# Spreading quadrant maxima as f32r high and low parts, at the end of a burst, in an induced-attention and maxout kernel

## Chip, cores and metric

The kernel runs on one core of one Trainium2 chip. The metric is the device time in microseconds of one execution; a lower number is better. The engines are named as in the profile: PE is TensorE (PEld its weight loads), DVE is VectorE, ACT is ScalarE, POOL is GpSimd, and SP issues DMAs.

## What is computed

Four batches of 12544 tokens with 128 channels go through two attention stages with 32 inducing rows, and the result through a maxout layer with three weight matrices and an output matrix. Everything is float32.

```python
B, N, m, C = (4, 12544, 32, 128)
def mab(q, kv):
    s = scale * (q @ kv.transpose(0, 2, 1))
    s = s - s.max(-1, keepdims=True)
    a = np.exp(s)
    a /= a.sum(-1, keepdims=True) + 1e-09
    return a @ kv
h = mab(I, x)              # 32 inducing rows attend over 12544 tokens
x = mab(x, h)              # 12544 tokens attend over 32 states
h = np.maximum(np.maximum(x @ w1, x @ w2), x @ w3)   # d_ff = 768
return h @ w_out
```

The first call of `mab` is called first attention here, the second one second attention.

## The kernel before

A batch is 98 tiles of 128 tokens: group 0 has 2 tiles, groups 1 to 6 have 16 each. The first attention of a group has its scores in one PSUM bank of 128 partitions: the tokens are split into four quadrants, and each quadrant holds the 32 inducing rows in its own 32 partitions. So an inducing row has four maxima, one in each quadrant, and they have to be put together before the exponential. `attend_max` (L292, VectorE) takes the negated maximum along each partition (`mq`, 128x1). `attend_column` (L299, ScalarE) multiplies the 0/1 matrix `quad` (128x4) with it (`md`, 128x4: the maximum stands in the column of its quadrant). `attend_spread` (L306, TensorE) is a float32 matmul of `md` with the 0/1 matrix `sel` (128x128), which gives every partition all four maxima of its inducing row. `attend_least` (L312, or L315 and L316) takes the least of the four and, from group 1 on, of the group before. Then come the exponential (`attend_weights`, L322, ScalarE), the factor for the older sums (`attend_scale`, L365), a transposition of 32x32 blocks (`attend_transpose`, L336, VectorE), and in a later burst the sums over tokens (`attend_sums`, L346, 16 pairs of small matmuls).

Batch 0's first attention is a phase of its own (`phase1_first`). After it, everything runs in slots, 150 a batch. A slot is one column block of 128 of the 768 maxout columns for one chunk of 512 tokens (256 in group 0). In slot s, `advance` issues on TensorE one product of slot s+1 (`pu`, L669) and one of slot s (`pv`, L675); ScalarE keeps max(pu, 0) (`ru`, L684) and rounds an older result to f32r (`hi`, L691); VectorE takes max(pv, ru) (`h`, L702); the rest `lo` = h - hi is made on GpSimd (L699), or on VectorE (L705) for the slots of a group of 24 that `LOWVEC` names, two slots later and behind that slot's `h`. `stage2` issues, six slots behind, the three products with the output matrix (L727 to L729, `hi` and `lo` with its high and low parts; one more, L726, at the start of a chunk). The banks `pu` and `pv` exist twice each: slot s+2 overwrites slot s. A float32 product on this kernel's operands with 4 or 512 columns shows as two records each in the profile; an f32r product is one.

While batch b goes through the slots, the first attention of batch b+1 (called n in the code) is laid between them by the table `plan`: `at(s, f, ...)` puts a function behind `advance` of slot s and before its `stage2`. s0 is the first slot of the group g, which has 24 slots. `burst(s0 + 2, *first)` puts several matmul groups side by side: scores of the second attention of batch b (`scores_products`, L585), scores of the first attention of batch n (`attend_products`, L282) and the sums of the group before (`attend_sums`). There is a second burst at s0 + 15 in some groups. `softmax1(n, g, s, wait)` lays the steps from the maximum to the transposition at s+2 to s+10, with s = s0 + 2 after a first burst; `wait` (0, or `LATE` = 12) moves the steps from the spread on. The order in which the code calls these is the order on each engine: all five engines run a hand-written order.

```python
at(s + 2, attend_max, b, gi)
at(s + 3, attend_column, b)
at(s + 6 + wait, attend_spread, b)
at(s + 7 + wait, attend_least, b, gi)
at(s + 8 + wait, attend_weights, b, gi)
```

Per batch n = 1, 2, 3 there are seven spreads: groups 0 and 1 from g = 1 (its first and second burst), groups 2, 3 and 4 from the first bursts of g = 2, 3 and 4, group 5 from the second burst of g = 4, and group 6 from the first burst of g = 5.

Of the kernel before, what the change touches and what calls it, by code (L numbers as in the profile page):

```python
# [8 lines left out]
F32 = mybir.dt.float32  # L9
F32R = mybir.dt.float32r  # L10
# [3 lines left out]
ALU = mybir.AluOpType  # L14
AX = mybir.AxisListType
# [10 lines left out]
def kernel(ctx, tc, x, xt, ind_t, w1, w2, w3, w_out, out):  # L26
    nc = tc.nc
# [3 lines left out]
    P = 128  # L31
    NT = N // P
    NJ = DF // P
    NQ = P // M
# [18 lines left out]
    ORDER = "a a a a b a a b 0 c d m b a b a b a p d b 1 c s b b b s S m b q 2 c s 3 c s d s s d s"  # L53
    STEPS2 = (3, 5, 7, 8, 9, 10, 11, 13, 14, 15)
    scale = 1.0 / float(C) ** 0.5
    LATE = 12
    LOWVEC = (23, 0, 15, 18)
    LOWLAST = (23, 0, 9, 15, 18)
    UW = 2 * DF + C
    UQ = UW // NQ  # L60
# [4 lines left out]
    while t0 < NT:  # L65
        nt = NT % GT if t0 == 0 and NT % GT else GT
        assert nt == GT or nt <= NQ
        g = dict(t0=t0, nt=nt, at=t0 * P)
        groups.append(g)
        t0 += nt  # L70
    NG = len(groups)

    const = ctx.enter_context(tc.tile_pool(name="const", bufs=1))
    xp = ctx.enter_context(tc.tile_pool(name="xp", bufs=2))
    xtp = ctx.enter_context(tc.tile_pool(name="xtp", bufs=7))
    wk = ctx.enter_context(tc.tile_pool(name="wk", bufs=2))
    bp = ctx.enter_context(tc.tile_pool(name="bp", bufs=2))
    hp = ctx.enter_context(tc.tile_pool(name="hp"))
    op = ctx.enter_context(tc.tile_pool(name="op", bufs=2))
# [3 lines left out]
    bank_a, bank_u, bank_v, bank_o = (  # L83
        [ps.tile([P, 512], F32, name=f"{n}{i}", tag=f"{n}{i}") for i in range(2)] for n in ("aux", "pu", "pv", "acc")
    )

    spare = [None]
# [37 lines left out]
    def first_loads():  # L125
# [11 lines left out]
    sel = const.tile([P, P], F32, name="sel")  # L137
    nc.vector.tensor_reduce(
        out=sel[:, :M], in_=ident.rearrange("p (q m) -> p m q", m=M), axis=AX.X, op=ALU.add
    )  # L140
    nc.vector.tensor_copy(
        out=sel[:, M:].rearrange("p (q m) -> p q m", m=M),
        in_=sel[:, :M].unsqueeze(1).to_broadcast([P, NQ - 1, M]),
    )
    quad = const.tile([P, NQ], F32, name="quad")
    nc.vector.tensor_reduce(out=quad, in_=ident.rearrange("p (q m) -> p q m", m=M), axis=AX.X, op=ALU.add)

# [90 lines left out]
    state = {}  # L238
# [63 lines left out]
    def attend_spread(b, bank=None):  # L302
# [2 lines left out]
        st["mp"] = bank or spare[0]  # L305
        nc.tensor.matmul(out=st["mp"][:, :NQ], lhsT=sel, rhs=st["md"], start=True, stop=True)  # L306

    def attend_least(b, gi):
        st = state[b]
        new, mp = st["mneg"][:, gi : gi + 1], st["mp"]  # L310
        if b == 0 or gi == 0:
            nc.vector.tensor_reduce(out=new, in_=mp[:, :NQ], axis=AX.X, op=ALU.min)  # L312
        else:

            nc.vector.tensor_reduce(out=mp[:, NQ : NQ + 1], in_=mp[:, :NQ], axis=AX.X, op=ALU.min)  # L315
            nc.vector.tensor_tensor(out=new, in0=mp[:, NQ : NQ + 1], in1=st["mneg"][:, gi - 1 : gi], op=ALU.min)  # L316

    def attend_weights(b, gi):
        w = groups[gi]["nt"] * M
# [78 lines left out]
    def phase1_first():  # L398
# [19 lines left out]
        half(1, 0)  # L418
        attend_spread(0, bank_o[0])
        attend_least(0, 0)  # L420
        half(1, 8)
        work(WORK[0])
        st = state[0]
        for gi in range(NG - 1):
            last = gi == NG - 2
            attend_products(0, gi + 1, bank_a[(gi + 1) % 2])
            attend_weights(0, gi)
            half(gi + 2, 0)
            attend_max(0, gi + 1)
            attend_column(0)  # L430
            half(gi + 2, 8)
            if gi > 0:
                attend_sums(0, gi - 1, bank_o[1])
                attend_keep(0, gi - 1)
            attend_transpose(0, gi)
            if not last:
                work(WORK[gi + 1][0])
            attend_spread(0, bank_o[0])
            attend_least(0, gi + 1)
            if gi == 3:  # L440
                transpose_w2()
            if last:
                prep_products()
            else:
                work(WORK[gi + 1][1])
# [261 lines left out]
    class Chunk:  # L707
# [7 lines left out]
        def low(self, k):  # L715

            if self.q is None or (self.gi == 1 and self.q == k == 0):
                return False
            return NJ * self.q + k in (LOWVEC if self.b + 1 < B else LOWLAST)

# [49 lines left out]
    def at(s, f, *args):  # L770
        plan[s].append((f, args))

    def softmax2(b, gi, *when):

        gen = []

        def step():
            if not gen:
                gen.append(scores_steps(b, gi))
            next(gen[0], None)  # L780

        for s in when:
            at(s, step)

    def softmax1(b, gi, s, wait=0):

        at(s + 2, attend_max, b, gi)
        at(s + 3, attend_column, b)
        at(s + 6 + wait, attend_spread, b)
        at(s + 7 + wait, attend_least, b, gi)  # L790
        at(s + 8 + wait, attend_weights, b, gi)
        if gi > 0:
            at(s + 9 + wait, attend_scale, b, gi)
        at(s + 10 + wait, attend_transpose, b, gi)

    def burst(s, *what):

        for f, *args in what:
            at(s, f, *args)

    for b in range(B):
        base = b * per_batch + short
        n = b + 1
        for g in range(1, NG):
            s0 = base + (g - 1) * WIN
            first, second = [], []
            if g + 1 < NG:

                if n == B:

                    if g % 2:
                        first += [(scores_products, b, k, bank_a[k % 2]) for k in (g + 1, g + 2) if k < NG]
                elif b > 0 or g > 1:
                    first.append((scores_products, b, g + 1, bank_a[0]))
                softmax2(b, g + 1, *(s0 + i for i in STEPS2))
            if n < B:

                if g == 1:
                    if n == 1:
                        at(s0 + 1, load_tokens, 1, 4)  # L820
                    at(s0 + 4, load_channels, n, 2)
                    first.append((attend_products, n, 0, bank_a[1]))
                    softmax1(n, 0, s0 + 2)
                    second += [(attend_products, n, 1, bank_a[1]), (attend_sums, n, 0)]
                    at(s0 + 16, attend_add, n, 0)
                    softmax1(n, 1, s0 + 15)
                    at(s0 + 16, load_tokens, n + 1, 0)
                    at(s0 + 20, load_channels, n, 3)
                elif g < NG - 2:
                    first += [(attend_products, n, g, bank_a[1]), (attend_sums, n, g - 1)]  # L830
                    at(s0 + 3, attend_add, n, g - 1)
                    softmax1(n, g, s0 + 2, 0 if g == NG - 3 else LATE)
                    at(s0 + 4, load_channels, n, g + 2)
                    more = g + 3
                    if more < NG:
                        at(s0 + 5, load_tokens, n, more)
                    else:
                        at(s0 + 5, load_tokens, n + 1, more - NG + 1)
                    if g == NG - 3:
                        second += [(attend_products, n, g + 1, bank_a[1]), (attend_sums, n, g)]  # L840
                        at(s0 + 16, attend_add, n, g)
                        softmax1(n, g + 1, s0 + 15)
                        at(s0 + 16, load_tokens, n + 1, 2)
                elif g == NG - 2:
                    first += [(attend_products, n, g + 1, bank_a[1]), (attend_sums, n, g)]
                    at(s0 + 3, attend_add, n, g)
                    softmax1(n, g + 1, s0 + 2)
                    at(s0 + 5, load_tokens, n + 1, 3)
                    second.append((attend_sums, n, g + 1))
                    at(s0 + 16, load_tokens, n + 1, 4)  # L850
                    at(s0 + 16, attend_add, n, g + 1)
                    at(s0 + 18, add_quadrants, ("state", n), bank_a[1])
                    at(s0 + 18, total_sums, ("state", n), bank_a[0])
                    at(s0 + 19, invert_total, ("state", n))
                    at(s0 + 19, combine_states, ("state", n), 1)
                    at(s0 + 21, combine_products, ("state", n), bank_a[0])
                    at(s0 + 22, combine_high, ("state", n))
                    at(s0 + 23, combine_low, ("state", n))
                    for r in range(NQ):
                        at(s0 + 25 + 3 * r, combine_rows, ("state", n), r)  # L860
                else:
                    first += [(scores_products, n, 1, bank_a[0]), (scores_products, n, 0, bank_a[1])]
                    softmax2(n, 1, *(s0 + i for i in STEPS2))
                    softmax2(n, 0, *(s0 + i for i in (4, 6, 8, 9, 10, 11, 12, 13, 14, 15)))
                    if n + 1 < B:
                        at(s0 + 18, start_batch, n + 1)
                        at(s0 + 18, load_channels, n + 1, 0)
                        at(s0 + 18, load_channels, n + 1, 1)
            burst(s0 + 2, *first)
            burst(s0 + 15, *second)  # L870
# [25 lines left out]
    with tc.manual_schedule(engines=MANUAL):  # L896
        phase1_first()
        st = state[0]
# [89 lines left out]
```

## Time and profile before

| | |
|---|---|
| time, three runs | 822.32, 822.78 (median), 823.0 us |
| span of the profiled execution | 821.3 us, 1.5 us under the median of the runs |
| granted clock of TensorE | 1.000 over the span |
| batch 0's first attention, before the slots | up to about 48 us |
| POOL | 650.1 us busy (79%) |
| DMA | 102.51 MB, mean 125 GB/s, 38.5% of 16 engines' time |

The page gives of each engine the busy time as a share of the span, and then the chain of work that ended last, followed back from the last instruction; its share of an engine says how much of the end that engine set. The profiled execution's own time is known by its span. In rows in order of time the columns are the start, the duration in us, engine, line, operation, output <- input, tile and form, and the count; in square brackets stands the idle time of the engine before it and what ended that.

### The profile page before, as it was taken

To read this page: it belongs to the slowest core of one execution; us is meant where nothing else is said; L and a number is where in the kernel's file an instruction comes from. 1 tells how busy PE (TensorE), PEld (TensorE's weight loads), DVE (VectorE), ACT (ScalarE), POOL (GpSimd) and SP (SyncE) were. 2 spreads that over 40 slices of the span, in tenths; PEclk is the share of its full clock that TensorE was granted. 3 is DMA by queue.
4 is the path that set the end of the run, shared out by engine and by line. 5 is a ranking of instruction groups with operands and counts; after the bars stand their busy time and mean duration, and the time that the engine had idled before them with its cause. 6 is when DMAs were issued, how large, how long until landed. Compare 5 with 4: busy or idle time off the path is not lost.

```text
span 821.3 us, 14725 instructions
## 1 busy us (share of the span) xinstructions
PE 809.0 (98%) x4604; PEld 634.0 (77%) x4604; DVE 627.4 (76%) x1090; ACT 743.5 (91%) x1558; POOL 650.1 (79%) x521
## 2 busy tenths in 40 slices
PE   7989999999999999999999999999999999999998
PEld 5757778778788787777778777877778788787886
DVE  4977778777787687787786877877778788778864
ACT  5779889898899898898999988989889899899996
POOL 1269779778799697787888977977879889888887
PEclk9999999999999999999999999999999999999999
DMA  8844534433443544344334352431223222222221
GB/s 325 310 137 151 188 88 161 161 120 107 136 139 121 154 154 162 84 162 159 110 106 142 116 205 83 159 119 58 63 80 89 71 78 77 65 81 76 63 78 52
DMA packets 44206, 102.51 MB, mean 125 GB/s; under 512 B 9568, under 2 KB 13536, under 8 KB 38880
## 3 DMA queue, kind: packets, MB, share of 16 engines
q1 hardware_dynamic: 43984, 101.44, 38.5%
q8 instruction: 37, 0.61, 0.3%
q14 instruction: 41, 0.34, 0.1%
q10 hardware_dynamic: 144, 0.13, 0.0%
HBM read 48.12 MB, written 25.69 MB: 90 GB/s over the span
## 4 chain that ended last, share of the span: by engine, by line
PE 95%; DMA 2%; DVE 1%; SPq 1%; ACT 1%; issue 0%; ACTq 0%; DVEq 0%
PE acc L727 17%; PE pv L675 16%; PE acc L728 16%; PE acc L729 16%; PE pu L669 16%; PE aux L585 3%; PE acc L726 3%; PE acc L346 3%; PE aux L282 2%; DMA xg<-in_x_dram 2%; PE acc L306 0%; PE pu L272 0%; SPq L100 0%; PE pv L272 0%; PE aux L551 0%; DMA pT<-pl 0%
## 5 line engine op out<-in xcount | busy, mean ns | idle before, releaser
L699 POOL TENSOR_TENSOR lo<-h,hi 128x512 fp32r<-128x512 f32 (+1 forms) x502 | 634.9, 1295 | 129.8 <-ACT hi L691 84.0
L702 DVE TENSOR_TENSOR h<-pv,ru 128x512 f32<-128x512 f32 (+1 forms) x600 | 404.2, 675 | 167.8 <-PE pv L675 81.2
L684 ACT ACTIVATE ru<-pu 128x512 f32<-128x512 f32 (+1 forms) x600 | 375.3, 626 | 52.6 <-PE pu L669 49.7
L691 ACT CAST hi<-h 128x512 fp32r<-128x512 f32 (+1 forms) x600 | 386.4, 644 | 0.4 <-DVE h L702 0.3
L727 PE MATMUL acc<-hi,wo_hi 128*128 128x512 f32 (+1 forms) x600 | 236.9, 395 | 0.0
L675 PE MATMUL pv<-pT,us 128*128 128x512 f32 (+1 forms) x600 | 232.1, 387 | 0.3 <-DVE h L702 0.3
L669 PE MATMUL pu<-pT,us 128*128 128x512 f32 (+1 forms) x600 | 231.5, 386 | 0.4 <-DMA pT<-pl 0.4
L728 PE MATMUL acc<-hi,wo_lo 128*128 128x512 f32 (+1 forms) x600 | 231.5, 386 | 0.0
L729 PE MATMUL acc<-lo,wo_hi 128*128 128x512 f32 (+1 forms) x600 | 231.2, 385 | 0.0
L727 PEld LDWEIGHTS acc<-hi,wo_hi 128*128 128x128 f32 x600 | 112.7, 188 | 30.0 <-issue 8.7
L675 PEld LDWEIGHTS pv<-pT,us 128*128 128x128 f32 x600 | 112.6, 188 | 24.2 <-DVE h L702 1.6
L669 PEld LDWEIGHTS pu<-pT,us 128*128 128x128 f32 x600 | 112.6, 188 | 23.9 <-DMA pT<-pl 0.6
L729 PEld LDWEIGHTS acc<-lo,wo_hi 128*128 128x128 f32 x600 | 112.7, 188 | 23.0
L728 PEld LDWEIGHTS acc<-hi,wo_lo 128*128 128x128 f32 x600 | 112.8, 188 | 21.1
L705 DVE TENSOR_TENSOR lo<-h,hi 128x512 fp32r<-128x512 f32 x98 | 71.3, 727 | 0.7 <-ACT hi L691 0.7
L744 ACT COPY o<-acc 128x512 f32<-128x512 f32 (+1 forms) x99 | 61.1, 617 | 0.0
L726 PE MATMUL acc<-pT,us 128*128 128x512 f32 (+1 forms) x100 | 38.7, 387 | 0.0
L346 PEld LDWEIGHTS acc<-xg,aT 128*32 128x32 f32 x768 | 21.1, 110 | 11.4 <-issue 6.8
L282 PE MATMUL aux<-xT,iT 128*32 128x512 f32 x192 | 25.3, 598 | 1.6 <-ACT xT L274 1.6
L346 PE MATMUL acc<-xg,aT 128*32 128x128 f32 x768 | 25.6, 274 | 0.0
L585 PE MATMUL aux<-xT,hT 128*32 128x512 f32 x192 | 25.1, 603 | 0.0
L192 POOL TENSOR_TENSOR rest<-rest,t 128x768 f32<-128x768 f32 x3 | 5.5, 1824 | 24.3 <-DVE rest L184 24.3
(119 smaller groups left out, 445.4 us busy)
## 6 DMA issues: line engine op xcount, KB each, us to landing
out_dram<-o SPq DMA_DIRECT2D x95, 256.0 KB, 2.0
xg<-in_x_dram SPq DMA_DIRECT2D x23, 1024.0 KB, 6.9
xT<-in_xt_dram SPq DMA_DIRECT2D x18, 1024.0 KB, 5.2
pT<-ph SPq DMA_DIRECT2D x192, 64.0 KB, 2.0
pT<-pl SPq DMA_DIRECT2D x192, 64.0 KB, 2.0
raw<-in_w_dram SPq DMA_DIRECT2D x3, 768.0 KB, 9.5
us<-uh SPq DMA_DIRECT2D x24, 52.0 KB, 1.9
us<-ul SPq DMA_DIRECT2D x24, 52.0 KB, 1.9
```

The source lines that it names most:

```text
L346: nc.tensor.matmul(out=hps[q * M : (q + 1) * M, :C], lhsT=aT[:, t * M : (t + 1) * M], rhs=xg[:, t, :], start=(t < NQ), stop=(t + NQ >= nt),)
L669: nc.tensor.matmul(out=pu[:, :w], lhsT=state[c.b]["us"][:, 2 * j * P : (2 * j + 1) * P], rhs=c.pT[:, :w], start=True, stop=True)
L675: nc.tensor.matmul(out=pv[:, : d.w], lhsT=state[d.b]["us"][:, (2 * j + 1) * P : (2 * j + 2) * P], rhs=d.pT[:, : d.w], start=True, stop=True,)
L684: nc.scalar.activation(out=ru[:, :w], in_=pu[:, :w], func=AF.Relu)
L691: nc.scalar.copy(out=hi[:, : c.w], in_=h[:, : c.w])
L699: nc.gpsimd.tensor_sub(**args)
L702: nc.vector.tensor_max(out=h[:, : d.w], in0=pv[:, : d.w], in1=relus.pop(s)[:, : d.w])
L705: nc.vector.tensor_sub(**low)
L726: nc.tensor.matmul(out=c.acc[:, :w], lhsT=us[:, 2 * DF :], rhs=c.pT[:, :w], start=True, stop=False)
L727: nc.tensor.matmul(out=c.acc[:, :w], lhsT=wo_hi[:, j, :], rhs=c.hh[j][:, :w], start=False, stop=False)
L728: nc.tensor.matmul(out=c.acc[:, :w], lhsT=wo_lo[:, j, :], rhs=c.hh[j][:, :w], start=False, stop=False)
L729: nc.tensor.matmul(out=c.acc[:, :w], lhsT=wo_hi[:, j, :], rhs=c.hl[j][:, :w], start=False, stop=(j == NJ - 1))
```

## The change

Batch 0's own first attention keeps the old functions. For batches 1 to 3 four things change.

1. The spread is done in f32r. ScalarE rounds quad * mq to f32r (the high part), VectorE takes the rest (the low part, a new instruction), and one f32r matmul of the 128x8 high and low parts with an f32r copy of `sel` (`sel_r`) replaces the float32 matmul of 128x4. A new reduction adds each pair before the least is taken.
2. In the first bursts of g = 2 to 5 the order is now: scores of batch n, maximum, high and low part, scores of the second attention of batch b, sums, spread (columns 256 on of the bank in which the sums stand). The least is taken in the next slot. The old separate steps of these four groups fall away; the spreads of groups 0, 1 and 5 stay where they were.
3. `LATE` goes from 12 to 8, so the exponential, factor and transposition of groups 2 and 3 come four slots earlier.
4. In `LOWVEC` slot 0 gives way to slot 21: the `lo` of slot 0 goes from VectorE to GpSimd, that of slot 21 from GpSimd to VectorE. In group 1 slot 0 was on GpSimd already.

```diff
-    LATE = 12
-    LOWVEC = (23, 0, 15, 18)
+    LATE = 8
+    LOWVEC = (21, 23, 15, 18)
...
+    sel_r = const.tile([P, P], F32R, name="sel_r")
+    nc.vector.tensor_copy(out=sel_r, in_=sel)
...
+    def running_column(b, gi):
+        st = state[b]
+        mr = st["mr"] = wk.tile([P, NQ, 2], F32R, name="mr", tag="mr")
+        nc.scalar.mul(out=mr[:, :, 0], in_=quad, mul=st["mq"])
+        nc.vector.scalar_tensor_tensor(
+            out=mr[:, :, 1], in0=quad, scalar=st["mq"], in1=mr.bitcast(F32)[:, :, 0], op0=ALU.mult, op1=ALU.subtract
+        )
+
+    def running_spread(b, col=0):
+        st = state[b]
+        mp = st["mp"] = spare[0][:, col : col + 4 * NQ]
+        nc.tensor.matmul(
+            out=mp[:, : 2 * NQ], lhsT=sel_r, rhs=st["mr"].rearrange("p q s -> p (q s)"), start=True, stop=True
+        )
+
+    def running_least(b, gi):
...
+        nc.vector.tensor_reduce(
+            out=quads, in_=mp[:, : 2 * NQ].rearrange("p (q s) -> p q s", s=2), axis=AX.X, op=ALU.add
+        )
...
-    def softmax1(b, gi, s, wait=0):
+    def softmax1(b, gi, s, wait=0, joined=False):
-        at(s + 2, attend_max, b, gi)
-        at(s + 3, attend_column, b)
-        at(s + 6 + wait, attend_spread, b)
-        at(s + 7 + wait, attend_least, b, gi)
+        if not joined:
+            at(s + 2, attend_max, b, gi)
+            at(s + 3, running_column, b, gi)
+            at(s + 6 + wait, running_spread, b)
+            at(s + 7 + wait, running_least, b, gi)
...
+    def joined(b, gi, *others):
+        return [
+            (attend_products, b, gi, bank_a[1]),
+            (attend_max, b, gi),
+            (running_column, b, gi),
+            *others,
+            (running_spread, b, 2 * P),
+        ]
...
-                    first += [(attend_products, n, g, bank_a[1]), (attend_sums, n, g - 1)]
+                    first = joined(n, g, *first, (attend_sums, n, g - 1))
+                    at(s0 + 3, running_least, n, g)
...
-                    first += [(attend_products, n, g + 1, bank_a[1]), (attend_sums, n, g)]
+                    first = joined(n, g + 1, *first, (attend_sums, n, g))
+                    at(s0 + 3, running_least, n, g + 1)
```

The lines of the changed kernel have other numbers; the names tell the rows. On TensorE, the first burst of g = 2 in batch 0's slots stood like this (aux_79 and aux_80 are the banks of the two kinds of scores, acc_86 the bank of the sums):

```order
L675 MATMUL pv_83<-pT,us 128x512
L585 MATMUL aux_79<-xT,hT 32x512 x4
L282 MATMUL aux_80<-xT,iT 32x512 x4
L346 MATMUL acc_86<-xg,aT 32x128 x16
L727 MATMUL acc_85<-hi,wo_hi 128x512
```

The same place in the changed kernel:

```order
L701 MATMUL pv_83<-pT,us 128x512
L284 MATMUL aux_80<-xT,iT 32x512 x4
L611 MATMUL aux_79<-xT,hT 32x512 x4
L372 MATMUL acc_86<-xg,aT 32x128 x16
L321 MATMUL acc_86<-mr,sel_r 128x8
L753 MATMUL acc_85<-hi,wo_hi 128x512
```

The two kinds of scores have changed places, and the spread, which stood 18 slots later by itself, now ends the burst. On VectorE, the rows around the same burst before (`h` of pv_83 beside lo belongs to the burst's slot):

```order
L705 TENSOR_TENSOR lo<-h,hi 128x512
L336 STREAM_TRANSPOSE aT<-a 128x512
L702 TENSOR_TENSOR h<-pv_83,ru 128x512
L705 TENSOR_TENSOR lo<-h,hi 128x512
L702 TENSOR_TENSOR h<-pv_84,ru 128x512
L598 STREAM_TRANSPOSE aux_79<-aux_79 128x512
L382 SCALAR_TENSOR_TENSOR hs<-hs,al,acc_86 128x128
L702 TENSOR_TENSOR h<-pv_83,ru 128x512
L292 TENSOR_REDUCE mq<-aux_80 128x1
```

And in the changed kernel:

```order
L731 TENSOR_TENSOR lo<-h,hi 128x512
L362 STREAM_TRANSPOSE aT<-a 128x512
L728 TENSOR_TENSOR h<-pv_83,ru 128x512
L294 TENSOR_REDUCE mq<-aux_80 128x1
L314 SCALAR_TENSOR_TENSOR mr<-quad,mq,mr 128x4
L728 TENSOR_TENSOR h<-pv_84,ru 128x512
L624 STREAM_TRANSPOSE aux_79<-aux_79 128x512
L329 TENSOR_REDUCE acc_86<-acc_86 128x4
L336 TENSOR_REDUCE acc_86<-acc_86 128x1
L337 TENSOR_TENSOR mneg<-acc_86,mneg 128x1
L408 SCALAR_TENSOR_TENSOR hs<-hs,al,acc_86 128x128
L728 TENSOR_TENSOR h<-pv_83,ru 128x512
```

The maximum and the low part (which waits for ScalarE's high part) now stand in the burst in the place of a `lo`, and three small rows stand in the slot after it. On ScalarE, later in the same group, around the output copy of slot 18, the rows before:

```order
L744 COPY o<-acc_85 128x512
L684 ACTIVATE ru<-pu_81 128x512
L691 CAST hi<-h 128x512
L684 ACTIVATE ru<-pu_82 128x512
L691 CAST hi<-h 128x512
```

And in the changed kernel:

```order
L770 COPY o<-acc_85 128x512
L348 ACTIVATE a,lst<-aux_80,mneg 128x512
L710 ACTIVATE ru<-pu_81 128x512
L717 CAST hi<-h 128x512
L391 ACTIVATE al<-mneg 128x1
L710 ACTIVATE ru<-pu_82 128x512
```

The exponential and the factor now stand directly behind that copy; before, they stood four slots later.

More of the change, by code (lines that the diff above doesn't have):

```diff
@@ L306, in attend_spread @@
         nc.tensor.matmul(out=st["mp"][:, :NQ], lhsT=sel, rhs=st["md"], start=True, stop=True)
+    def running_column(b, gi):
[12 more added lines that the diff above has]
+    def running_least(b, gi):
+        st = state[b]
+        new, mp = st["mneg"][:, gi : gi + 1], st["mp"]
+        quads = mp[:, 2 * NQ : 3 * NQ]
+        nc.vector.tensor_reduce(
+            out=quads, in_=mp[:, : 2 * NQ].rearrange("p (q s) -> p q s", s=2), axis=AX.X, op=ALU.add
+        )
+        if gi == 0:
+            nc.vector.tensor_reduce(out=new, in_=quads, axis=AX.X, op=ALU.min)
+            return
+        least = mp[:, 3 * NQ : 3 * NQ + 1]
+        nc.vector.tensor_reduce(out=least, in_=quads, axis=AX.X, op=ALU.min)
+        nc.vector.tensor_tensor(out=new, in0=least, in1=st["mneg"][:, gi - 1 : gi], op=ALU.min)
     def attend_least(b, gi):
@@ L310, in attend_least @@
         new, mp = st["mneg"][:, gi : gi + 1], st["mp"]
[L311 to L316, printed above, removed]
+        nc.vector.tensor_reduce(out=new, in_=mp[:, :NQ], axis=AX.X, op=ALU.min)
     def attend_weights(b, gi):
@@ L829 @@
                 elif g < NG - 2:
-                    first += [(attend_products, n, g, bank_a[1]), (attend_sums, n, g - 1)]
+                    first = joined(n, g, *first, (attend_sums, n, g - 1))
+                    at(s0 + 3, running_least, n, g)
                     at(s0 + 3, attend_add, n, g - 1)
-                    softmax1(n, g, s0 + 2, 0 if g == NG - 3 else LATE)
+                    softmax1(n, g, s0 + 2, 0 if g == NG - 3 else LATE, True)
                     at(s0 + 4, load_channels, n, g + 2)
@@ L844 @@
                 elif g == NG - 2:
-                    first += [(attend_products, n, g + 1, bank_a[1]), (attend_sums, n, g)]
+                    first = joined(n, g + 1, *first, (attend_sums, n, g))
+                    at(s0 + 3, running_least, n, g + 1)
                     at(s0 + 3, attend_add, n, g)
-                    softmax1(n, g + 1, s0 + 2)
+                    softmax1(n, g + 1, s0 + 2, 0, True)
                     at(s0 + 5, load_tokens, n + 1, 3)
```

## The prediction

> **What bounds the kernel now.** I read the page's busy times and chain first, then a batch-long window, then the order of time on TensorE.
>
> ```profile
> PE 809.0 (98%) x4604; PEld 634.0 (77%) x4604; DVE 627.4 (76%) x1090; ACT 743.5 (91%) x1558; POOL 650.1 (79%) x521
> PE 95%; DMA 2%; DVE 1%; SPq 1%; ACT 1%; issue 0%; ACTq 0%; DVEq 0%
> 250.00:445.00 195.00, 195.00 (x1109) 152.75 (x1109) 151.09 (x266) 179.52 (x380) 160.33 (x128) 1.00 0.43 136
> ```
>
> The chain that ended last is 95% TensorE, and in the window of one whole batch (250 to 445 us) TensorE is busy 195.00 of 195.00 us at granted clock 1.00. Busy alone proves little for pipelined matmuls, so I looked at starts. Two matmuls of 512 columns start 0.227 us apart, and in the batches this spacing holds except around short or narrow matmuls. So inside a batch, time taken out of TensorE's row comes out of the end, as long as ScalarE (91%) and VectorE stay ahead of the reuse of their PSUM buffers.
>
> **What one separate spread costs.** The order of time on TensorE, then its weight loads, around the spread of batch 1, group 2:
>
> ```profile
> 110.31 0.39 PE L675 MATMUL pv<-pT,us 128*128 128x512 f32 x1
> 110.53 0.28 PE L306 MATMUL acc<-md,sel 128*128 128x4 f32 x2
> 110.67 0.48 PE L727 MATMUL acc<-hi,wo_hi 128*128 128x512 f32 x1
> 110.99 0.40 PE L728 MATMUL acc<-hi,wo_lo 128*128 128x512 f32 x1
> ...
> 110.31 0.41 PEld L306 LDWEIGHTS acc<-md,sel 128*128 128x128 f32 x2
> 110.64 0.19 PEld L727 LDWEIGHTS acc<-hi,wo_hi 128*128 128x128 f32 x1
> ```
>
> From pv to L728 are 110.99 - 110.31 = 0.68 us; without the spread it would be 2 x 0.227 = 0.454. The f32 spread therefore costs 0.227 us. It is two records (x2), each with its own load of 128x128 weights; the four columns hide no load, so two loads stand bare, 0.114 us each: the second of the spread and that of L727. A second place checks the reading:
>
> ```profile
> 205.75 0.39 PE L675 MATMUL pv<-pT,us 128*128 128x512 f32 x1
> 205.98 0.30 PE L391 MATMUL aux<-sel,hs 128*128 128x32 f32 x2
> 206.12 0.39 PE L504 MATMUL aux<-sel,lst 128*128 128x32 f32 x2
> 206.34 0.48 PE L726 MATMUL acc<-pT,us 128*128 128x512 f32 x1
> 206.66 0.40 PE L727 MATMUL acc<-hi,wo_hi 128*128 128x512 f32 x1
> ```
>
> Four short records cost 206.66 - 205.75 - 0.454 = 0.456, again 0.114 each, and the load left bare at the end belongs to an f32r matmul. So a bare load costs 0.114 whether f32 or f32r.
>
> **Step 1, f32r in place of f32.** The f32r spread is one matmul of 8 columns with one load. No row shows one so short. Its cost lies between nothing (its load and the next hidden) and the 0.227 of the f32 pair; I take 0.114, one bare load of the following matmul, the nearest row. It saves 0.113 each. The source view counts them:
>
> ```profile
> L306 PE MATMUL acc<-md,sel x56: 167/252/273, 6.8 to 584.2; 128*128 128x4 f32 x56
> L292 DVE TENSOR_REDUCE mq<-aux x28: 203/680/692, 6.0 to 580.6; 128x1 f32<-128x512 f32 x24, 128x1 f32<-128x64 f32 x4
> L315 DVE TENSOR_REDUCE acc<-acc x18: 158/160/161, 82.6 to 587.1; 128x1 f32<-128x4 f32 x18
> L382 DVE SCALAR_TENSOR_TENSOR hs<-hs,al,acc x18: 303/307/340, 92.1 to 595.9; 128x128 f32<-128x128 f32 x18
> ```
>
> 56 records are 28 spreads; 7 are batch 0's own (unchanged), so 21 change: 21 x 0.113 = **2.4 us saved**.
>
> By the Trainium skill, "FP8 and Floating Point Precision", section TensorE Precision Notes, a true f32 matmul makes four passes and reduced-precision f32 needs no such split. The trace shows two records with two loads, so for four columns I count loads; counting passes is a rival below.
>
> **Step 2, twelve spreads move into the burst.** Four per batch (groups 2, 3, 4 and 6) now end the first burst. There the spread's load takes the place that L727's has now, after the last 32-column matmul, and L727's load is bare behind it: again 0.114, already in the sum. What is new is a wait on TensorE: spread needs products, maximum, ScalarE's high part, VectorE's low part. Behind it in TensorE's row stand the whole second product, pu and pv. A burst now, groups 3 and 4 like this one:
>
> ```profile
> 117.90 1.07 PE L585 MATMUL aux<-xT,hT 128*32 128x512 f32 x8
> 118.18 0.68 DVE L702 TENSOR_TENSOR h<-pv,ru 128x512 f32<-128x512 f32 x1
> 118.78 1.04 PE L282 MATMUL aux<-xT,iT 128*32 128x512 f32 x8
> 119.64 1.06 PE L346 MATMUL acc<-xg,aT 128*32 128x128 f32 x32
> 120.62 0.19 PEld L727 LDWEIGHTS acc<-hi,wo_hi 128*128 128x128 f32 x1 [0.20 <-issue]
> 122.17 0.69 DVE L702 TENSOR_TENSOR h<-pv,ru 128x512 f32<-128x512 f32 x1 [2.70 <-issue]
> 123.63 0.68 DVE L702 TENSOR_TENSOR h<-pv,ru 128x512 f32<-128x512 f32 x1
> 125.11 0.39 PE L675 MATMUL pv<-pT,us 128*128 128x512 f32 x1
> ```
>
> With the new batch's scores first, they end at about 117.90 + 1.07 = 118.97, and h leaves VectorE at 118.86. The links' hops are in phase 1:
>
> ```profile
> 34.66 0.68 DVE L292 TENSOR_REDUCE mq<-aux 128x1 f32<-128x512 f32 x1
> 35.38 0.30 ACT L299 ACTIVATE md<-quad,mq 128x4 f32<-128x4 f32 x1 [0.60 <-DVE mq L292]
> 35.73 0.39 PE L306 MATMUL acc<-md,sel 128*128 128x4 f32 x2 [0.65 <-ACT md L299]
> ```
>
> Each hop is 0.04 to 0.05. The low part (128x4) is in no row: between 0.16 (L315) and 0.31 (L382, 128 columns); I take 0.17, being four columns. From the end of the scores: 0.05 + 0.68 + 0.04 + 0.30 + 0.04 + 0.17 + 0.05 = 1.33, so the operand is there at 120.30, or 120.44 by the longer row. TensorE wants it at 120.62: **0.2 to 0.3 us to spare**. VectorE idles 2.70 us there, which hides the maximum, the low part and the wait for ScalarE that now blocks its queue; the next h comes only at 122.17.
>
> In groups 2 and 6 the transposition of the weights comes first:
>
> ```profile
> 86.55 1.06 PE L585 MATMUL aux<-xT,hT 128*32 128x512 f32 x8
> 87.46 0.65 DVE L702 TENSOR_TENSOR h<-pv,ru 128x512 f32<-128x512 f32 x1
> 88.04 0.67 DVE L705 TENSOR_TENSOR lo<-h,hi 128x512 fp32r<-128x512 f32 x1
> 89.28 0.19 PEld L727 LDWEIGHTS acc<-hi,wo_hi 128*128 128x128 f32 x1 [0.20 <-issue]
> ```
>
> The maximum takes the place of the lo at 88.04 (that lo, slot 0, goes to GpSimd). Then 88.04 + 0.68 + 0.04 + 0.30 + 0.04 + 0.17 + 0.05 = 89.32 against 89.28: late by 0.04, by the longer row 0.18. Six such bursts: 0.2 to 1.1 us lost. I take **0.4 us**, nearer the short row.
>
> By the Trainium skill, "TensorE: Matmul & The Clock Gate", section Step-by-step: what each phase is for, only weight loads are pulled ahead and matmuls stay in program order. No row here tests that with a late spread.
>
> **Step 3, around it.** Per spread VectorE gains the low part and one reduction (0.16), some 0.33; the separate maximum leaves the step after next, so what queues there stays equal. One slot after the burst three small rows, 0.5 us together, stand ahead of the h that began at 123.63; it then ends at 124.8, and the pv that reuses its bank starts at 125.11 (both in the burst's rows above): covered by 0.3 us. In groups 2 and 3 the exponential comes four slots earlier (LATE), and its transposition falls behind the lo of slot 18:
>
> ```profile
> 110.80 0.69 DVE L702 TENSOR_TENSOR h<-pv,ru 128x512 f32<-128x512 f32 x1 [0.44 <-PE pv L675]
> 111.41 0.68 DVE L705 TENSOR_TENSOR lo<-h,hi 128x512 fp32r<-128x512 f32 x1
> 112.21 0.69 DVE L702 TENSOR_TENSOR h<-pv,ru 128x512 f32<-128x512 f32 x1
> 113.95 0.39 PE L675 MATMUL pv<-pT,us 128*128 128x512 f32 x1
> 116.22 0.70 DVE L336 STREAM_TRANSPOSE aT<-a 128x512 f32<-128x512 f32 x1
> 116.97 0.69 DVE L702 TENSOR_TENSOR h<-pv,ru 128x512 f32<-128x512 f32 x1
> ```
>
> h, lo, aT, h at 110.8 to 111.0, +0.61, +0.61, +0.75 puts the second h at 112.8 to 113.0 and its end at 113.5 to 113.7. The pv that overwrites its bank starts at 113.95 - 0.23 = 113.72 (no spread ahead of it any more). It just fits: I cost it at nothing; without that cover it is up to 0.2 us at six places, 1.2 us. The lo rows (slot 0 to GpSimd, slot 21 to VectorE) lie on engines at 76 and 79% and are used six slots later: nothing. One copy (sel_r) before the first maximum lies in VectorE's wait for data: nothing. No DMA is added or moved in its queue.
>
> **Sum.** Against the profiled execution: span 821.3 - 2.4 + 0.4 = 819.3. The timed runs are 822.78 in the median, 1.5 us above that span, and I keep this distance: 822.78 - 2.0 = **820.8 us**, a gain of 0.24%. A measurement here tells from no change about 0.2%, 1.65 us, so the limits are 821.1 and 824.4.
>
> **Rivals.**
> - Thin margins break: the six late bursts at 0.18 and the six h at 0.2 cost 1.1 + 1.2 = 2.3 us instead of 0.4. For it: both margins are below 0.2 us. Against: I counted the longest rows. Time 822.78 - 2.4 + 2.3 = 822.7; halfway, 821.7. Both "same". Chance 0.26.
> - The other side: VectorE's maximum is let go one group late, when the second scores in the burst have ended too. By the burst's rows they end 0.88 later (118.78 against 117.90), so in groups 3 and 4 the operand is there at 121.18, 0.56 late, and about as late in groups 2 and 6: 12 x 0.56 = 6.7, and 822.78 - 2.4 + 6.7 = 827.1. It turns slower than before by more than the limit when each of the 12 waits exceeds 4.0/12 = 0.34 us. For it: the products share a semaphore count. Against: the h at 118.18 starts while the burst's first products still run, so VectorE is let go within a burst. Chance 0.06.
> - The passes, not the loads, make the price: three quarters of 0.227 go, 21 x 0.170 = 3.6, with the 0.4 lost 819.6. Against: the 0.114 per load fits both places with 4 and 32 columns. Chance 0.07; the four passes of the Trainium skill named above would give this.
> - The forecast, 819.9 to 821.1: chance 0.61.
>
> **How the numbers follow.** Faster: 0.61 + 0.07, less a little because 820.8 lies 0.3 from the limit: 0.64. Same: 0.29. Slower: 0.07. The range runs from the cheap spread, 819.4, to both thin margins broken, 822.6; it leaves out the late maximum and a tail on each side.
>
> **What would show it.** Right: one record per spread; from pv to L728 at a separate one 0.57 instead of 0.68; bursts of groups 3 and 4 with L727's load 0.11 later than now and no wait of TensorE for mr. Wrong: TensorE waiting for mr in a burst by more than 0.2, a gap between matmuls about slot 21 to 23 of groups 2 and 3, or a separate spread still at 0.2.

## The result and the profile after

The changed kernel takes 829.0 us in the median of four runs (828.54 to 829.25), the kernel before 822.58 (822.32 to 823.0). The medians are 6.4 us apart; the ratio on record is 1.0072, with a 95% interval from 1.0055 to 1.0089, so the change makes the kernel slower by some 0.7%, where 820.8 was forecast. The span of the profiled execution went from 821.3 to 826.9 us.

The page of the changed kernel first, busy times and the chain that ended last:

```profile
PE 809.6 (98%) x4583; PEld 630.6 (76%) x4583; DVE 652.4 (79%) x1136; ACT 744.0 (90%) x1558; POOL 649.6 (79%) x518
PE 89%; DVE 5%; ACT 3%; DMA 2%; issue 1%; SPq 1%; DVEq 0%; ACTq 0%
```

TensorE has 21 records and 21 weight loads less, as meant, but its share of the chain fell from 95% to 89%, and VectorE and ScalarE have 8% of it in place of 2%: TensorE now waits for them. The view of waits names the place:

```profile
PEld acc L321 <- DVE mr L314: 8.7, 12, 0.9
PE acc L321 <- DVE mr L314: 5.4, 12, 0.6
ACT mr L313 <- DVE mq L294: 5.1, 12, 0.5
DVE mr L314 <- ACT mr L313: 4.5, 13, 0.4
```

The columns are the total in us, the times and the longest. L321 is the new spread, L314 VectorE's low part. Twelve spreads wait, as many as stand in bursts. The source view of L314 then gives the surprise, its minimum, median and maximum in ns:

```profile
L314 DVE SCALAR_TENSOR_TENSOR mr<-quad,mq,mr x21: 274/879/1147, 61.1 to 581.7; 128x4 fp32r<-128x4 f32 x21
```

An instruction on 128x4 takes 0.88 us, more than one on 128x512. The order of time in the burst of g = 3 (as at 117.58 to 120.97 us before), all engines but the plain products:

```profile
117.95 1.06 PE L284 MATMUL aux<-xT,iT 128*32 128x512 f32 x8
118.51 2.52 POOL L725 TENSOR_TENSOR lo<-h,hi 128x512 fp32r<-128x512 f32 x2 [1.21 <-ACT hi L717]
119.08 0.69 DVE L294 TENSOR_REDUCE mq<-aux 128x1 f32<-128x512 f32 x1 [0.21 <-PE aux L284]
119.81 0.30 ACT L313 ACTIVATE mr<-quad,mq 128x4 fp32r<-128x4 f32 x1 [0.37 <-DVE mq L294]
120.14 0.91 DVE L314 SCALAR_TENSOR_TENSOR mr<-quad,mq,mr 128x4 fp32r<-128x4 f32 x1 [0.37 <-ACT mr L313]
121.10 0.19 PEld L321 LDWEIGHTS acc<-mr,sel_r 128*128 128x128 f32 x1 [0.62 <-DVE mr L314]
121.10 0.27 PE L321 MATMUL acc<-mr,sel_r 128*128 128x8 f32 x1 [0.36 <-DVE mr L314]
121.23 0.48 PE L753 MATMUL acc<-hi,wo_hi 128*128 128x512 f32 x1
```

Up to the high part the chain runs nearly as worked out in the prediction: the maximum starts 0.07 us after the scores, and the next two hops are 0.04 and 0.03. Then L314 ends at 121.05, and GpSimd's two `lo` end at 118.51 + 2.52 = 121.03. This is no chance of one burst: in this trace all 21 low parts, in bursts and at separate places, end 0.02 us after a `lo` of GpSimd.

Where the time is lost is seen slot by slot: the starts of the 600 pv of one trace less those of the other, and the jumps in this difference. From the first pv to the last the changed kernel loses 6.4 us; its first pv comes 0.9 us earlier than before, so the spans differ by 5.6. (Over the experiments below the start of the first pv moves between 1.0 us earlier and 2.3 later, so the jumps are a finer measure than the times.) Each row below is the jump in us per place, with the number of places; the bursts of g = 2 and 5 are those of groups 2 and 6.

| place | after less before | without low part (e1) | separate, no low part (e3) |
|---|---|---|---|
| burst of g = 3, 4, spread joined (6) | +0.50 | +0.10 | 0 |
| burst of g = 2, 5, spread joined (6) | +0.73 | +0.09 | 0 |
| old places of these spreads (12) | -0.24 | -0.24 | -0.11 |
| spreads from second bursts, slot 21 or 22 (6) | +0.15 | -0.11 | -0.11 |
| spread of group 0 (3) | +0.26, -0.12, -0.11 | -0.12 | -0.11 |
| slot 15 of g = 4, 5 (6) | +0.09 | +0.09 | 0 |
| end of a batch, seen at slot 5 of the next (3) | +0.09 | +0.09 | 0 |
| sum from first to last slot | +6.4 | -1.5 | -1.9 |

The bursts lose 6 x 0.50 + 6 x 0.73 = 7.4 us, of which a bare load is 0.1 each and the rest, 6.2, is waiting. The nine spreads outside these bursts gain 1.0 us in e1 and lose 0.9 here: another 1.9.

### The profile page after: what moved, and what is told of

Read it like the earlier page. It is cut to its first block, busy times and chain, and to the rows that moved or that the text cites. A ratio compares the mean times of both kernels' runs of the same rounds, so it can differ in the third digit from the quotient of the medians.

```text
span 826.9 us, 14735 instructions
## 1 busy us (share of the span) xinstructions
PE 809.6 (98%) x4583; PEld 630.6 (76%) x4583; DVE 652.4 (79%) x1136; ACT 744.0 (90%) x1558; POOL 649.6 (79%) x518
## 4 chain that ended last, share of the span: by engine, by line
PE 89%; DVE 5%; ACT 3%; DMA 2%; issue 1%; SPq 1%; DVEq 0%; ACTq 0%
PE acc L753 16%; PE pv L701 16%; PE pu L695 16%; PE acc L754 16%; PE acc L755 16%; PE acc L752 3%; PE aux L284 2%; DMA xg<-in_x_dram 2%; PE acc L372 1%; PE aux L611 1%; DVE mr L314 1%; DVE mq L294 1%; DVE h L728 1%; ACT hi L717 1%; DVE aT L362 1%
## 5 line engine op out<-in xcount | busy, mean ns | idle before, releaser
L731 DVE TENSOR_TENSOR lo<-h,hi 128x512 fp32r<-128x512 f32 x101 | 75.8, 750 | 1.6 <-ACT hi L717 1.6
L294 DVE TENSOR_REDUCE mq<-aux 128x1 f32<-128x512 f32 (+1 forms) x28 | 17.3, 616 | 8.5 <-PE aux L284 7.5
```

What stands on the lines that cost most here:

```text
L731: nc.vector.tensor_sub(**low)
```

## The experiments

The theory: the low part reads two tensors from SBUF, and it is held until the `lo` that GpSimd is running, which reads SBUF too, has ended. Its rivals: the chain is too long for the burst in any case; the row is slow in itself; the short f32r matmul is not cheaper. All times below stand beside runs of the kernel before on the same chip.

**e1, the low part left out.**

```diff
-        nc.vector.scalar_tensor_tensor(
-            out=mr[:, :, 1], in0=quad, scalar=st["mq"], in1=mr.bitcast(F32)[:, :, 0], op0=ALU.mult, op1=ALU.subtract
-        )
...
-            out=mp[:, : 2 * NQ], lhsT=sel_r, rhs=st["mr"].rearrange("p q s -> p (q s)"), start=True, stop=True
+            out=mp[:, :NQ], lhsT=sel_r, rhs=st["mr"], start=True, stop=True
...
-        nc.vector.tensor_reduce(
-            out=quads, in_=mp[:, : 2 * NQ].rearrange("p (q s) -> p q s", s=2), axis=AX.X, op=ALU.add
-        )
```

> The changed kernel without VectorE's low part and without the reduction that adds the pairs; the spread is f32r with the rounded maximum alone, 4 columns. Since every partition of an inducing row gets the same rounded values and the softmax does not depend on the shift, the output stays that of the reference. Theory (the low part, with two SBUF inputs, is held until GpSimd's running lo ends, and TensorE waits for it in 12 bursts): no wait of TensorE for mr, every first burst with a spread 0.11 us longer than before instead of 0.50 to 0.74, 821 us or a little less. Rival 1 (the chain of maximum, hop, high part, hop is too long for the burst by itself): waits of 0.2 us and more stay in groups 2 and 6 at least, 822.5 to 825 us. Rival 2 (a short f32r spread is not cheaper than the f32 one): no wait, but 822.5 us.

Measured: 821.37 us, ratio 0.9981 (0.9968 to 0.9993). The waits for the low part are gone (one weight load still waits 0.2 us for the high part), and the joined bursts are 0.09 to 0.10 longer than before in all four groups. Taking this one instruction and its follower, the reduction of the pairs, out is worth 7.6 us against the changed kernel. The chain up to the high part is not too long, and the f32r spread is cheaper: the first and the third rival fall. Which of the two rows costs, and why, is left to e2, which keeps both.

**e2, the same instruction with one operand from PSUM.**

```diff
-            out=mr[:, :, 1], in0=quad, scalar=st["mq"], in1=mr.bitcast(F32)[:, :, 0], op0=ALU.mult, op1=ALU.subtract
+            out=mr[:, :, 1], in0=st["a"][gi][:, :NQ], scalar=st["mq"], in1=mr.bitcast(F32)[:, :, 0], op0=ALU.mult, op1=ALU.subtract
```

> The changed kernel with one operand of the low part taken from the scores' bank in PSUM instead of quad in SBUF: same instruction, same place, same waits, one SBUF input; its values are meaningless. Theory (two SBUF inputs against GpSimd's lo): the row falls from a median of 0.88 us to 0.35 or less, TensorE waits less than 0.2 us in groups 2 and 6 and not at all in groups 3 and 4, 820.5 to 821.8 us. Rival (the row is slow in itself, by its f32r output, its pointer or its wait for ScalarE): it stays at 0.8 us and more and the time at 828.5 to 829.3.

The low part then holds other values than the rest of the maximum; the run serves for its times alone. Measured: 821.82 us, ratio 0.9989 (0.9975 to 1.0003). The burst of g = 3 in its order of time, and below it the source view:

```profile
118.10 2.52 POOL L725 TENSOR_TENSOR lo<-h,hi 128x512 fp32r<-128x512 f32 x2 [1.20 <-ACT hi L717]
...
118.66 0.69 DVE L294 TENSOR_REDUCE mq<-aux 128x1 f32<-128x512 f32 x1 [0.21 <-PE aux L284]
119.39 0.30 ACT L313 ACTIVATE mr<-quad,mq 128x4 fp32r<-128x4 f32 x1 [0.37 <-DVE mq L294]
119.72 0.22 DVE L314 SCALAR_TENSOR_TENSOR mr<-aux,mq,mr 128x4 fp32r<-128x4 f32 x1 [0.37 <-ACT mr L313]
120.26 0.19 PEld L321 LDWEIGHTS acc<-mr,sel_r 128*128 128x128 f32 x1 [0.20 <-issue]
120.26 0.27 PE L321 MATMUL acc<-mr,sel_r 128*128 128x8 f32 x1
...
L314 DVE SCALAR_TENSOR_TENSOR mr<-aux,mq,mr x21: 200/222/224, 61.7 to 575.1; 128x4 fp32r<-128x4 f32 x21
```

GpSimd runs the same two `lo` at the same moment, and the low part takes 0.22 us instead of 0.91, ends at 119.94 and has 0.3 us to spare before TensorE's load. Its 21 rows lie between 0.200 and 0.224. So neither its output, its pointer nor its wait for ScalarE makes it slow: the second rival falls. The added reduction, which stands here too, is not what costs.

**e6, GpSimd kept idle there.**

```diff
-    LOWVEC = (21, 23, 15, 18)
+    LOWVEC = (0, 1, 23, 15, 18)
```

> The changed kernel as it is, low part and all from SBUF, but with LOWVEC (0, 1, 23, 15, 18): the lo of slots 0 and 1, which GpSimd runs while the low part waits in the burst, are made on VectorE instead, so GpSimd has nothing to do there. Theory (the partner that holds the low part is GpSimd's lo): the low part falls to 0.3 us or less in the bursts of groups 3, 4 and mostly 2, 6, and stays at about 1 us at the separate places. VectorE's lo of slot 0 now stands ahead of the maximum, which comes 0.6 later, so the wait of TensorE hardly shrinks: 827 to 829.5. Rival (the low part is slow for another reason): 0.8 us in the bursts as before, and the chain then 0.6 later still, 12 x 0.6 more: over 833.

Measured: 840.2 us, ratio 1.0224 (1.0205 to 1.0243). The burst of g = 3, in which GpSimd has no row now, and the source view:

```profile
121.11 0.68 DVE L731 TENSOR_TENSOR lo<-h,hi 128x512 fp32r<-128x512 f32 x1
121.71 0.68 DVE L294 TENSOR_REDUCE mq<-aux 128x1 f32<-128x512 f32 x1
122.42 0.30 ACT L313 ACTIVATE mr<-quad,mq 128x4 fp32r<-128x4 f32 x1 [1.01 <-DVE mq L294]
122.75 0.22 DVE L314 SCALAR_TENSOR_TENSOR mr<-quad,mq,mr 128x4 fp32r<-128x4 f32 x1 [0.37 <-ACT mr L313]
...
L314 DVE SCALAR_TENSOR_TENSOR mr<-quad,mq,mr x21: 223/224/1212, 62.0 to 592.9; 128x4 fp32r<-128x4 f32 x21
```

With both operands in SBUF again, the low part takes 0.22 us in all 12 bursts and 1.08 to 1.21 at the nine separate places, where GpSimd runs and where it again ends 0.02 us after a `lo` of GpSimd. This is the other half of e2: one SBUF input is enough to free it, and an idle GpSimd is enough too. The time lies 10.7 us above the upper end of the expectation. The joined bursts cost what they cost in the changed kernel (0.49 and 0.77), as expected, since the `lo` ahead of the maximum delays the chain; but the two `lo` put on VectorE there also delay `h`, with gaps of 0.1 to 0.6 us at slots 6 to 8 of five groups a batch, some 9 us that the expectation did not count.

**e3, f32r in the old places, without low part.** Nothing but the matmul's type differs from the kernel before (`running_column`, `running_spread` and `running_least` as in e1, called where `softmax1` called the old ones; no join, old tables).

```diff
-        at(s + 3, attend_column, b)
-        at(s + 6 + wait, attend_spread, b)
-        at(s + 7 + wait, attend_least, b, gi)
+        at(s + 3, running_column, b, gi)
+        at(s + 6 + wait, running_spread, b)
+        at(s + 7 + wait, running_least, b, gi)
```

> The kernel before, with only the 21 spreads of batches 1 to 3 in f32r (rounded maximum alone, 4 columns), in their old places: no join, old burst order, LATE 12, old LOWVEC. Theory (a short record costs one bare weight load of 0.114 us): each spread 0.114 instead of 0.227, 822.6 - 2.4 = 820.2, at most 0.5 of it given back by ScalarE's thin margin late in the groups 4 and 5. Rival (f32r not cheaper): 822.6.

Measured: 820.74 us, ratio 0.9971 (0.9960 to 0.9981). The spread that stood at 110.53 before, in the order of time on TensorE:

```profile
110.00 0.39 PE L700 MATMUL pv<-pT,us 128*128 128x512 f32 x1
110.23 0.17 PE L318 MATMUL acc<-mr,sel_r 128*128 128x4 f32 x1
110.26 0.48 PE L752 MATMUL acc<-hi,wo_hi 128*128 128x512 f32 x1
110.58 0.40 PE L753 MATMUL acc<-hi,wo_lo 128*128 128x512 f32 x1
```

From pv to the second of the following products are 0.58 us, against 0.68 before and 0.454 without a spread: one bare load instead of two. All 21 places gain 0.10 to 0.13. This is the lowest time measured here; e8 below has the same sum of jumps, -1.9 us.

**e11, the same kernel again, beside e9 and e10 below.**

> The separate kernel without low part again (f32r spreads in the old places and nothing else), timed beside the two joined ones: 820.7 us as before. If the place in the burst were worth anything by itself, e9 would lie under it by more than 0.5 us; the theory says that it does not, since one bare weight load is paid in either place.

Measured: 821.95 us, ratio 0.9988 (0.9976 to 1.0000). The trace shows the same 21 gains, but the timed runs spread from 820.45 to 823.88 here. The gain of this version is real in the traces and, by the two measurements, between nothing and 0.4%.

**e4, joined, but the spread in float32 (4 columns, no low part).**

```diff
-        mr = st["mr"] = wk.tile([P, NQ], F32R, name="mr", tag="mr")
+        mr = st["mr"] = wk.tile([P, NQ], F32, name="mr", tag="mr")
...
-            out=mp[:, :NQ], lhsT=sel_r, rhs=st["mr"], start=True, stop=True
+            out=mp[:, :NQ], lhsT=sel, rhs=st["mr"], start=True, stop=True
```

The diff is against e1.

> The changed kernel's places and order, but the spread as a float32 matmul of 4 columns without low part. Theory (a record is a bare load, and the place in the burst saves nothing by itself): each spread costs 0.227 wherever it stands, the operand is in time, so 822.6 within 0.5 us. Rival (the place at the burst's end hides one of the loads): 12 x 0.114 = 1.4 us less, 821.2. Rival (the place itself is harmful: longer chain, other order of scores): over 823.5.

Measured: 823.33 us, ratio 1.0007 (0.9993 to 1.0022). A joined burst is 0.20 to 0.22 longer, an old place 0.22 to 0.24 shorter: the two bare loads cost the same in either place. The place at the burst's end saves nothing by itself; all of the saving is f32r's.

**e5, f32r high and low parts in the old places.** As e3, with the low part as in the changed kernel.

> The kernel before with the 21 spreads in f32r high and low parts in their old places: the low part on VectorE reads quad and the high part from SBUF as in the changed kernel, but no burst waits for it. Theory (the low part is held by GpSimd's lo and then holds VectorE's own queue): it takes 0.7 to 1.1 us at most places, TensorE does not wait for mr, but h comes late behind it: against the same kernel without low part (820.7) up to 0.25 us at each of the second-burst places, and 0 to 0.3 at the 12 others; 822 to 825. Rival (only the wait in the burst costs): 820.7 to 821.2.

Measured: 824.17 us, ratio 1.0024 (1.0015 to 1.0034). The low part takes 0.275 to 1.133 us, median 0.886, and no matmul waits for it; yet the kernel is 3.4 us slower than e3. The source view:

```profile
L314 DVE SCALAR_TENSOR_TENSOR mr<-quad,mq,mr x21: 275/886/1133, 61.1 to 583.1; 128x4 fp32r<-128x4 f32 x21
```

Jumps against the kernel before stand at the places behind it: +0.14 at the second-burst spreads (e3: -0.11), +0.08 to +0.11 at slot 9 of g = 2 and 3, +0.14 at slot 15 of g = 4 and 5. Held by GpSimd, the low part holds VectorE's queue, the next `h` comes late, and the pv that needs its bank waits (0.2 to 0.4 us of its weight load at slots 9 and 21). At slot 15 it is the pu that waits, 0.3 us, for ScalarE's `ru`; that the late `h` reaches ScalarE there, through its `hi`, is likely but not shown. The rival (only the wait in the burst costs) falls.

**e8 and e7, the tables.** Both are e1 with a table undone: e8 with LATE 12, e7 with LATE 12 and LOWVEC (23, 0, 15, 18).

> The joined kernel without low part, with LATE 12 alone undone. Theory (LATE moves work that has margin in either place): as without the low part, 821.4 within 0.4 us, and no new gap about slots 20 to 23. Rival (the earlier exponential is what makes the joined kernel 0.6 us slower than the separate one): 820.8.

Measured: 821.26 us, ratio 0.9990 (0.9979 to 1.0002), with the jumps of e1 at the same places to 0.01 us. Without the low part, LATE costs and brings nothing.

> The joined kernel without low part, with both old tables (LATE 12, LOWVEC 23, 0, 15, 18). Theory (with the low part gone neither table is what costs; old LOWVEC puts the lo of slot 0 ahead of the maximum in the burst, 0.6 later): the 0.09 us lost at the end of each batch goes (that is the lo of slot 21 on VectorE), but TensorE waits 0.1 to 0.6 in the joined bursts: 822 to 825. Rival (the margin of the burst covers it): 820.7.

Measured: 823.13 us, ratio 1.0011 (0.9998 to 1.0024). The 0.09 at each batch's end is gone; the bursts of g = 2 and 5 are 0.51 longer, so TensorE waits 0.4 there, but those of g = 3 and 4 stay at 0.10: there the margin covers a `lo` ahead of the maximum. The expectation had the wait in all four.

**e10 and e9, to get back what e1 gives back.** e10 is e1 with LOWVEC (23, 15, 18); e9 has in addition the exponential four slots earlier in the joined groups of g = 4 and 5.

```diff
-                    softmax1(n, g, s0 + 2, 0 if g == NG - 3 else LATE, True)
+                    softmax1(n, g, s0 + 2, -4 if g == NG - 3 else LATE, True)
...
-                    softmax1(n, g + 1, s0 + 2, 0, True)
+                    softmax1(n, g + 1, s0 + 2, -4, True)
```

> As e9, but with the exponential where the joined kernel has it. Theory: the 0.09 us at each batch's end goes, the 0.09 at slot 15 of two groups a batch stays: 0.3 under the joined kernel without low part and 0.5 above e9, about 820.6.

> The joined kernel without low part, LOWVEC (23, 15, 18) (the lo of slot 21 back on GpSimd), and in the groups whose maximum is joined in g = 4 and 5 the exponential, factor and transposition four slots earlier, which the join allows since the least is known one slot after the burst. Theory (of the 2.4 us that f32r takes out, the joined kernel gives back 0.09 us at slot 15 of these groups, where ScalarE's margin is used up, and 0.09 at each batch's end, where the lo of slot 21 fills VectorE): both go, 822.6 - 2.7 + 0.1 = 820.0, at or just under the separate kernel. Rival (the give-back at slot 15 has another cause, or returns at another slot): 820.8 to 821.4.

Measured: e10 822.19 us, ratio 0.9992 (0.9979 to 1.0005); e9 823.26, ratio 1.0002 (0.9992 to 1.0013). Both lie above their expectation and above e1. The batch ends lose nothing in either, as expected. But both show a new single gap of 1.0 us about slot 23 of g = 3 in batch 0, where pv waits for `h`; e9 has another of 0.6 us at slots 5 and 6 of g = 6 in batch 3, behind a `lo` on VectorE that took 1.68 us and ended 0.55 us after one of GpSimd. And e9's loss of 0.09 at slot 15 came back as 0.16 at slot 11 in five places of six. What gives back the 0.09 is seen in e1 at slot 15, ScalarE's row and TensorE's:

```profile
164.42 0.63 ACT L764 COPY o<-acc 128x512 f32<-128x512 f32 x1
164.89 0.65 ACT L704 ACTIVATE ru<-pu 128x512 f32<-128x512 f32 x1
165.61 0.49 PE L689 MATMUL pu<-pT,us 128*128 128x512 f32 x1
```

and in the view of waits of the same stretch, 160 to 167.5 us:

```profile
PEld pu L689 <- ACT ru L704: 0.2, 1, 0.2
```

The `ru` ends at 165.54, just when the pu that overwrites its bank should start. The reading, which no run tests by itself: the spread that stood at slot 8 no longer gives ScalarE 0.24 us, and its margin is used up. It fits that moving the exponential only moves the place, and that in e3, where each spread still takes 0.11 there, no gap opens. Ahead of the single gap of 1.0 us VectorE stood idle for 0.97 us (in e10) before a `lo` that waited for a `hi` of ScalarE; why it had to wait there is open.

## Why the prediction was wrong

**The step that failed** is in step 2, the sentence "The low part (128x4) is in no row: between 0.16 (L315) and 0.31 (L382, 128 columns); I take 0.17, being four columns". It was 0.72 to 0.91 us in the bursts; 0.17 was short even of the 0.22 that it takes when nothing holds it, but the 0.5 to 0.7 of the hold is what the sum had left out. The bounds came from rows that read at most one tensor from SBUF: L315 and L382 read PSUM. The rows of the kernel before held the right neighbour, VectorE's `lo`, which also takes two tensors from SBUF, in the source view of L705:

```profile
L705 DVE TENSOR_TENSOR lo<-h,hi x98: 671/681/1194, 76.5 to 814.3; 128x512 fp32r<-128x512 f32 x98
```

A maximum of 1194 ns for an instruction whose median is 681 is the mark of a holder: each of the 16 rows of L705 over 700 ns ends 0.55 us after a `lo` of GpSimd. For 128x4 the hold is no smaller, since it is the rest of GpSimd's instruction (1.3 us in the mean) and not a share of its own work. By the Trainium skill, "SBUF — State Buffer", section Who interferes with whom, a VectorE instruction with two SBUF inputs contends with a GpSimd instruction that reads SBUF, and one with at most one SBUF input, outside VectorE's two-port modes, does not. e2 and e6 agree on both halves: 0.22 us with one input, 0.22 with GpSimd idle, 0.7 to 1.2 in most rows with both.

The edit of LOWVEC belongs to the same step. The prediction put slot 0's `lo` on GpSimd at no cost; it is one of the two that GpSimd runs in the burst. No run leaves it on VectorE with the low part in place. Before the change GpSimd had one `lo` in the burst of g = 3:

```profile
119.56 1.27 POOL L699 TENSOR_TENSOR lo<-h,hi 128x512 fp32r<-128x512 f32 x1 [2.38 <-ACT hi L691]
```

It ended at 120.83, after the 120.62 at which TensorE wants the operand. So this one alone would have held the low part too long, by this estimate.

**The sum's other terms.** The price of a short f32r spread, 0.114, was right (e3: 0.10 to 0.13 saved, 21 times, with 4 columns; e5: 0.11 with 8 columns, at the eight places where nothing behind comes late), and so was the count of loads rather than passes. The chain without the hold was right: 1.33 us were worked out from the end of the scores, and in e2 the burst of g = 3 had 0.3 to spare and those of g = 2 and 5 came late by 0.03 at most places, where 0.04 was said. A place in the burst costs about the same loads as anywhere (e4). The rival of the passes would have saved 0.17 a place and falls with e3; the rival of the thin margins falls with e2 and e1, where the late bursts lose 0.03 (once 0.11) and the `h` about slot 21 nothing. The thin margin about slot 21, costed at nothing, held (e1, e8).

**Two terms were missing.** The hold costs a second time at separate places, mostly through VectorE's queue (e5: 3.4 us for 21 low parts; in the changed kernel some 1.9 us for nine). And 0.8 us of what f32r brings is given back: 0.09 six times to ScalarE's margin at slot 15, and 0.09 three times at batch ends, where the `lo` of slot 21, said to cost nothing, stands on VectorE (gone in e7, e9 and e10). A `lo` of VectorE is held there too: in e1 it takes 1.28 us and ends 0.55 after one of GpSimd.

**The rivals.** The one on the other side had the place and nearly the time (12 waits in bursts, 827.1) but not the mechanism: the maximum was not let go late; it starts 0.07 after its scores. That the time came near is luck. Its chance of 0.06 was worked out for that mechanism alone.

## What to carry to other kernels

Before an instruction is added to VectorE, count its inputs in SBUF: with two of them, a GpSimd busy with SBUF tensors can hold it for the rest of its own instruction, however small it is, and the price is to be read from two-input rows, at their maximum. A small instruction at the end of a chain across engines, in front of an in-order queue that bounds the kernel, is to be costed by the time that it takes when held, and not by its free one. Here the best low part was none: a softmax's shift need only be the same for all that share it.

## What the runs showed that was not expected

A 128x4 instruction on VectorE takes between 0.22 and 1.21 us in one trace (e6), and which of the two depends on what GpSimd does. And the same low part costs where no matmul waits for it, 3.4 us in e5, mostly because what stands behind it in VectorE's queue comes late. The bare weight load of 0.11 us, two for a float32 spread and one for an f32r one, was expected and held.
